# One attention and mixture-of-experts kernel: a ninth column in the gate, integer rank sums, single indirect transfers in two steps, and later weight splits

## The chip, the core and the metric

One NeuronCore of a Trainium2 chip runs the whole program. The metric is the device time of one execution in microseconds. TensorE (PE) multiplies matrices, VectorE (DVE), ScalarE (ACT) and GpSimd (POOL) work element by element, SyncE (SP) issues the plain transfers, and GpSimd issues the indirect ones (scatter and gather by a list of row numbers).

## The reference, cut to what matters

A decaying linear attention over 4 sequences of 768 positions with 8 heads of 48 features gives 3072 rows of 384 features. Each row goes to the one of 8 experts with the largest logit, in order of arrival, up to the capacity of 768 rows an expert, and comes back weighted with the softmax probability of that expert.

```python
state = w * state + k[t] v[t]^T ;  x[t] = r[t] (state_before + u k[t] v[t]^T)
logits = x @ w_gate ;  e = argmax(logits)
z = exp(logits - max) ;  gate = z[e] / (z.sum() + 1e-09)
out[i] = gate[i] * (relu(x[i] @ w1[e]) @ w2[e])      # if the expert still has room
```

At the largest logit z is 1, so the gate is the reciprocal of the sum of z plus 1e-09.

## The kernel before, in words

**Attention.** The 3072 rows are 24 tiles of 128 positions, 6 for each sequence. The loop over `i` (lines 621 to 695) is a software pipeline written out by hand: the order of the calls is the order of the instructions on each engine, and nothing reorders them. Step `i` computes the scores of tile `i + 1` (line 525), masks them (529), scales the keys of tile `i + 3` (511, one product over both halves of the transposed loads), multiplies on GpSimd (495), mixes (81, 83), pulls the tile's logits out (93, 94), updates the state (537, 547), and computes the values of tile `i` (559, 568). ScalarE scales the identity with the bonus of tile `i + 2` (506), copies the values out (572) and writes finished rows into a row buffer (111, 112). There are three row buffers, one for each group of tiles in turn. The last step of a sequence has no state update.

**Routing.** Tiles are routed in groups of two, the last two tiles alone (`GROUPS`, line 33). `route` (125 to 167) is a generator in three parts, and `advance` runs one part at a time. Part one finds the first largest logit and subtracts the maximum. Part two takes the exponential on ScalarE, sums ranks by matmul and adds the group's counts to `lane` on GpSimd (152). Part three (160 to 166) multiplies rank and one-hot mark, sums them into a float, casts to the integer `slot`, sums z, adds 1e-9 and takes the reciprocal. The group's tiles then join `todo`, and `scatters(n)` issues for the first n of them an indirect transfer on GpSimd's queue, which writes 128 rows of 400 words into the sorted array `xsd` in HBM. A step issues one, so a tile is scattered four steps after its values.

**Experts.** Nine sets: the first expert's rows in two halves of 208 (`SETS`, line 26), then one set of 416 for each other expert. `gather(k)` reads a set's rows back, 104 rows an instruction; `xtrans` transposes them on TensorE (300) and splits them into a high and a low part (304 on ScalarE, 305 on VectorE). `layer1` has 8 blocks of 9 matmuls (317 to 319) with a Relu on ScalarE (322) and its low part on VectorE (323) behind each; `layer2` has 3 blocks of 24 matmuls (334 to 336) and a copy (337). The first half of the first expert may use only rows of the first 16 tiles (`SNAP`), so its gather can run before the loop ends. Its first layer's blocks 0 to 3 (called `first` to `fourth`) stand between the last routing parts.

**Weights.** `wstream` is a generator too: each `next(ws)` fetches raw weights on SP's queue into one of four buffers and splits one piece, high part on ScalarE (250), low part on VectorE (251). Pieces 0 to 5 are the first layer's (512 wide), 6 to 13 the second layer's (384 wide). The second expert's weight buffers take the place of the attention's tiles, among them the row buffers that the scatters read.

**Flags.** `flags` (201 to 215) is nine short VectorE instructions and a cast; its result decides at the very end whether a branch for rare inputs runs.

## Time and profile before

| what | value |
|---|---|
| median of three runs | 390.99 us (390.31 to 391.17) |
| the profiled execution's own time | 391.63 us |
| its span (first to last instruction) | 389.9 us |
| mean granted TensorE clock | 0.986 |
| busy: PE, DVE, ACT, POOL | 373.2, 241.3, 204.0, 138.5 us |
| HBM read, written | 52.58 MB, 10.03 MB |

The profile is of one execution, which took 0.64 us more than the median. A busy time counts pipelined instructions as a whole, so a high share of TensorE doesn't say that it runs at its peak. The granted clock is the share of full speed that TensorE was given. In a timeline a row says when an instruction (or a run of like ones, with their count) began, how long it took, the engine, the line, the operation, what it writes and reads, and in brackets how long the engine stood idle before it and what ended that. The engine named there is the last one by the profile; where it had long been done, another wait ended the idle time.

### The profile page before, as it was taken

Reading aid. Unit: us, or ns where it says so; the run is one execution under the profiler, and the core shown is the slowest. Engines: PE = TensorE matmul, PEld = TensorE weight load, DVE = VectorE, ACT = ScalarE, POOL = GpSimd, SP = SyncE. Lnnn points to the kernel's source line nnn. Section 1 sums busy time; section 2 is a strip of 40 time slices with the busy share of each in tenths; the row PEclk is TensorE's granted clock in tenths of the full one; section 3 lists DMA queues with packets and bytes.
Section 4 is the critical chain, followed back from the end, with each engine's and each line's share of the span. In section 5 each row is a group of like instructions: output and inputs, shape, how many; then the busy total and the mean of one; then the engine's idle time right before and its main releaser. Section 6 shows DMA issues by size and latency. Waiting matters only on the chain.

```text
span 389.9 us, 9402 instructions
## 1 busy us (share of the span) xinstructions
PE 373.2 (96%) x3569; PEld 336.3 (86%) x3570; DVE 241.3 (62%) x615; ACT 204.0 (52%) x565; POOL 138.5 (36%) x199
## 2 busy tenths in 40 slices
PE   8999999999999888999999999999999999999993
PEld 3678787787786777999999999999999999999992
DVE  6899999999996656735546546545545645643310
ACT  3668896778787424616525525525625624622301
POOL 7124656575554237402502602602602601201203
PEclk9999999999999996999999999999999999999998
DMA  7848878687812555642743643643644644400102
GB/s 299 329 140 285 282 233 305 233 287 245 262 64 72 151 178 160 183 129 73 209 129 110 197 135 110 185 137 118 187 131 132 185 129 134 137 3 16 43 3 71
DMA packets 20950, 62.51 MB, mean 160 GB/s; under 512 B 3996, under 2 KB 4132, under 8 KB 20896
## 3 DMA queue, kind: packets, MB, share of 16 engines
q1 hardware_dynamic: 15120, 46.74, 38.3%
q0 software_dynamic: 5632, 14.56, 11.6%
q8 instruction: 30, 0.49, 0.5%
q10 hardware_dynamic: 144, 0.52, 0.4%
q14 instruction: 24, 0.20, 0.2%
HBM read 52.58 MB, written 10.03 MB: 161 GB/s over the span
## 4 chain that ended last, share of the span: by engine, by line
PE 60%; issue 14%; DVE 13%; ACT 8%; POOL 2%; DMA 1%; POOLq 1%; ACTq 0%; DVEq 0%
PE a L317 8%; PE a L318 8%; PE a L319 7%; PE b L334 7%; PE b L336 7%; PE b L335 7%; ACT s L506 5%; DVE s L529 4%; PE y L568 3%; PE a L525 2%; PE warm L463 2%; PE yp L350 2%; POOL out L342 2%; PE tp L300 2%; DVE dm L511 2%
## 5 line engine op out<-in xcount | busy, mean ns | idle before, releaser
L342 POOL DMA_INDIRECT out<-yo,ids x32 | 32.4, 1013 | 163.2 <-ACT yo L341 161.6
L317 PE MATMUL a<-xh,ws 128*128 128x416 f32 (+1 forms) x216 | 74.7, 346 | 0.1
L334 PE MATMUL b<-hh,ws 128*128 128x416 f32 (+2 forms) x208 | 72.5, 348 | 2.2 <-ACT hh L322 2.2
L322 ACT ACTIVATE hh<-a 128x416 fp32r<-128x416 f32 (+1 forms) x72 | 34.6, 480 | 72.8 <-PE a L319 69.4
L319 PE MATMUL a<-xh,ws 128*128 128x416 f32 (+1 forms) x216 | 72.1, 334 | 0.0
L318 PE MATMUL a<-xl,ws 128*128 128x416 f32 (+1 forms) x216 | 71.9, 333 | 0.0
L335 PE MATMUL b<-hl,ws 128*128 128x416 f32 (+2 forms) x208 | 70.8, 340 | 0.2 <-DVE hl L323 0.2
L336 PE MATMUL b<-hh,ws 128*128 128x416 f32 (+2 forms) x208 | 70.6, 339 | 0.0
L251 DVE TENSOR_TENSOR ws<-wr,ws 128x384 fp32r<-128x384 f32 (+1 forms) x112 | 67.1, 615 | 5.3 <-ACT ws L250 5.0
L323 DVE SCALAR_TENSOR_TENSOR hl<-a,hh 128x416 fp32r<-128x416 f32 (+1 forms) x72 | 39.0, 542 | 46.3 <-ACT hh L322 35.3
L506 ACT ACTIVATE s<-eye,l 128x128 f32<-128x128 f32 x168 | 53.8, 392 | 18.4 <-DVE l L94 18.2
L250 ACT CAST ws<-wr 128x384 fp32r<-128x384 f32 (+1 forms) x112 | 60.2, 557 | 5.6 <-DMA xsd<-xr,slot 5.6
L337 DVE COPY yt<-b 128x416 f32<-128x416 f32 (+2 forms) x26 | 14.2, 545 | 66.7 <-PE b L336 64.5
L495 POOL TENSOR_TENSOR P<-dm 112x512 f32<-112x512 f32 x21 | 26.8, 1276 | 48.0 <-PE a L525 13.8
L334 PEld LDWEIGHTS b<-hh,ws 128*128 128x128 f32 x208 | 40.4, 194 | 2.6 <-ACT hh L322 2.4
L317 PEld LDWEIGHTS a<-xh,ws 128*128 128x128 f32 x216 | 40.8, 189 | 0.9 <-issue 0.5
L275 POOL DMA_INDIRECT xg<-xsd,pidx x32 | 35.2, 1101 | 17.4 <-issue 8.1
L318 PEld LDWEIGHTS a<-xl,ws 128*128 128x128 f32 x216 | 40.8, 189 | 0.5 <-DVE xl L305 0.2
L335 PEld LDWEIGHTS b<-hl,ws 128*128 128x128 f32 x208 | 40.3, 194 | 1.1 <-DVE hl L323 0.8
L319 PEld LDWEIGHTS a<-xh,ws 128*128 128x128 f32 x216 | 40.7, 188 | 0.1
L336 PEld LDWEIGHTS b<-hh,ws 128*128 128x128 f32 x208 | 40.3, 194 | 0.3
L304 ACT CAST xh<-tp 128x416 fp32r<-128x416 f32 (+1 forms) x27 | 12.3, 472 | 49.9 <-PE tp L300 44.7
(145 smaller groups left out, 580.4 us busy)
## 6 DMA issues: line engine op xcount, KB each, us to landing
wr<-w SPq DMA_DIRECT2D x24, 512.0 KB
wr<-w SPq DMA_DIRECT2D x32, 384.0 KB
dm<-dmj SPq DMA_DIRECT2D x23, 512.0 KB
bd<-bdc SPq DMA_DIRECT2D x24, 384.0 KB
dm<-dmj ACTq DMA_DIRECT2D x1, 512.0 KB
xg<-xsd,pidx POOLq DMA_INDIRECT x32
out<-yo,ids POOLq DMA_INDIRECT x32
xsd<-xr,slot POOLq DMA_INDIRECT x24
```

Of the source, the lines that this page charges most:

```text
L250: nc.scalar.copy(out=hi, in_=r)
L251: low.append(lambda: nc.vector.tensor_tensor(out=lo, in0=r, in1=hi.bitcast(F32), op=ALU.subtract))
L275: nc.gpsimd.indirect_dma_start(out=xg[k % 2][:, i].bitcast(I32), out_offset=None, in_=xsd[:, :], in_offset=bass.IndirectOffsetOnAxis(ap=pi ...
L317: nc.tensor.matmul(a, lhsT=wh, rhs=xh[:, d, o], start=d == 0, stop=False)
L318: nc.tensor.matmul(a, lhsT=wh, rhs=xl[:, d, o], start=False, stop=False)
L319: nc.tensor.matmul(a, lhsT=wl, rhs=xh[:, d, o], start=False, stop=d == 2)
L323: nc.vector.scalar_tensor_tensor(out=hl[:, f, o], in0=a, scalar=0.0, in1=hh[:, f, o].bitcast(F32), op0=ALU.max, op1=ALU.subtract)
L334: nc.tensor.matmul(y, lhsT=wh, rhs=hh[:, f, o], start=f == 0, stop=False)
L335: nc.tensor.matmul(y, lhsT=wh, rhs=hl[:, f, o], start=False, stop=False)
L336: nc.tensor.matmul(y, lhsT=wl, rhs=hh[:, f, o], start=False, stop=f == 7)
L342: r = nc.gpsimd.indirect_dma_start(out=out[:, :], out_offset=bass.IndirectOffsetOnAxis(ap=ids[k][0][:qo, i:i + 1], axis=0), in_=yo, in_off ...
L506: nc.scalar.mul(out=s[:, h, p], in_=eye, mul=bon)
```

## The change

Part three of `route` sums rank times mark straight into the integer `slot`, so the float `sf` and the cast go. The exponentials lie in the first eight of nine columns of a tile `zb`, two of which are used in turn; the ninth column is set to 1e-9 once, by GpSimd, and the sum runs over nine columns, so the addition goes. In steps 20 and 21 of the loop the place of the scatter is taken by one gather each of the first set's two; the end of step 20 no longer empties `todo` and gathers. Four calls of `next(ws)` behind blocks 4 to 7 of the first set's first layer go, one is put behind the second block of its second layer, and `flags` moves there too. The remaining pieces of the second expert follow in the second half's layers, whose loops already call `next(ws)`. The branch for dropped tokens, which runs only when an expert overflows, copies `slot` back to floats.

```diff
--- before.py
+++ after.py
@@ -61,7 +61,7 @@
         fl = const.tile([1, E + 4], I32, name="fl")
         okw = const.tile([128, 1], BF16, name="okw")
         slot = const.tile([128, NI], I32, name="slot")
-        sf = const.tile([128, NI], F32, name="sf")
+        zb = const.tile([128, 2, 4, E + 1], F32, name="zb")
 
         def disjoint(key, r):
             tc.declare_no_dep(r.ins, group=key, reason="rows of one scatter are rows of no other")
@@ -137,7 +137,8 @@
             nc.vector.tensor_reduce(out=km, in_=key, axis=AX.X, op=ALU.max)
             oh = sm.tile(sh, BF16, tag="oh", name=f"oh{gi}")
             nc.vector.tensor_tensor(out=oh, in0=key, in1=km.unsqueeze(2).broadcast_to(sh), op=ALU.is_equal)
-            z = sm.tile(sh, F32, tag="z", name=f"z{gi}")
+            zz = zb[:, gi % 2, 0:n]
+            z = zz[:, :, 0:E]
             nc.vector.tensor_tensor(out=z, in0=l, in1=mxb, op=ALU.subtract)
             yield 1
             nc.scalar.activation(z, z, AF.Exp)
@@ -158,11 +159,10 @@
                 rank = pen
             ps = sm.tile(sh, F32, tag="ps", name=f"ps{gi}")
             nc.vector.tensor_tensor(out=ps, in0=rank, in1=oh, op=ALU.mult)
-            nc.vector.tensor_reduce(out=sf[:, i0:i0 + n], in_=ps, axis=AX.X, op=ALU.add)
-            nc.vector.tensor_copy(out=slot[:, i0:i0 + n], in_=sf[:, i0:i0 + n])
+            with nc.allow_low_precision(reason="one of eight terms is not zero, a whole number below 2^24"):
+                nc.vector.tensor_reduce(out=slot[:, i0:i0 + n], in_=ps, axis=AX.X, op=ALU.add)
             zs = sm.tile([128, n], F32, tag="zs", name=f"zs{gi}")
-            nc.vector.tensor_reduce(out=zs, in_=z, axis=AX.X, op=ALU.add)
-            nc.vector.tensor_scalar(out=zs, in0=zs, scalar1=1e-9, scalar2=None, op0=ALU.add)
+            nc.vector.tensor_reduce(out=zs, in_=zz, axis=AX.X, op=ALU.add)
             nc.vector.reciprocal(out=xr[:, 0:n, DM + 1], in_=zs)
             todo.extend((i, xr[:, i - i0], nd) for i in range(i0, i0 + n))
 
@@ -269,9 +269,9 @@
 
             ids = {}
 
-            def gather(k):
+            def gather(k, tiles=None):
                 q, m = QT, SETS[k][2]
-                for i in range(m):
+                for i in tiles or range(m):
                     nc.gpsimd.indirect_dma_start(out=xg[k % 2][:, i].bitcast(I32), out_offset=None, in_=xsd[:, :],
                                                  in_offset=bass.IndirectOffsetOnAxis(ap=pidx[:q, k, i:i + 1], axis=0),
                                                  bounds_check=E * NT - 1, oob_is_err=False)
@@ -440,6 +440,7 @@
                     nc.gpsimd.memset(lane[:, 0, e:e + 1], float(e * NT // 128))
                     nc.gpsimd.memset(top[:, e:e + 1], float(e * NT + min(cap, NT)))
                     nc.gpsimd.memset(lim[:, e:e + 1], float(e * NT + min(cap, W1S)))
+                nc.gpsimd.memset(zb[:, :, :, E], 1e-9)
                 ii = sup.tile([128, NI], I32, name="ii")
                 nc.gpsimd.iota(ii, pattern=[[C, NI]], base=0, channel_multiplier=1)
                 nc.gpsimd.tensor_copy(out=idf, in_=ii)
@@ -648,7 +649,10 @@
                     each(scores, i + 1)
                 each(prep_keys, i + 3)
                 each(product, i + 3)
-                scatters(1)
+                if i in (20, 21):
+                    gather(0, [i - 20])
+                else:
+                    scatters(1)
                 c = mix(T[i + 2]["P"] if i + 2 < NI else None, T[i - 1]["xs"], ps1)
                 ct = mixed(c, wk)
                 update(i)
@@ -687,9 +691,6 @@
                     setup_ok(wc)
                 if i == 18:
                     early_places(sm, ps1)
-                if i == 20:
-                    scatters(NI)
-                    gather(0)
                 if i in (9, 13):
                     nc.gpsimd.memset(xg[i == 13], 0.0)
                 T.pop(i - 1)
@@ -735,12 +736,12 @@
             next(ws)
             for f in range(4, 8):
                 layer1(0, f)()
-                next(ws)
-            flags(sm)
             layer2(0, 0, columns(0))
             next(ws)
             gather(2)
             layer2(0, 1, columns(0))
+            next(ws)
+            flags(sm)
             take(1)
             for d in range(3):
                 xtrans(1, d)()
@@ -912,6 +913,8 @@
         def drop():
             with tc.tile_pool(name="dw", bufs=1) as dw:
                 rk = dw.tile([128, NI], F32, name="drk")
+                sf = dw.tile([128, NI], F32, name="dsf")
+                nc.vector.tensor_copy(out=sf, in_=slot)
                 nc.vector.tensor_copy(out=rk, in_=sf)
                 for e in range(1, E):
                     ge = dw.tile([128, NI], F32, tag="dge", name=f"dge{e}")
```

## Rows read from the trace of the kernel before

**Rows 1.** The chain that ended last, its shares by engine.

```profile
PE 60%; issue 14%; DVE 13%; ACT 8%; POOL 2%; DMA 1%; POOLq 1%; ACTq 0%; DVEq 0%
```

**Rows 2.** Timeline of PE, scores: start, us, engine, line, op, out<-in, count [idle before].

```profile
38.52 1.16 PE L525 MATMUL a<-dm 48*128 48x128 f32 x16
...
42.78 1.16 PE L525 MATMUL a<-dm 48*128 48x128 f32 x16
...
56.88 1.16 PE L525 MATMUL a<-dm 48*128 48x128 f32 x16
...
61.61 1.16 PE L525 MATMUL a<-dm 48*128 48x128 f32 x16
...
107.30 1.16 PE L525 MATMUL a<-dm 48*128 48x128 f32 x16
```

**Rows 3.** Timelines of DVE and POOL, line 165 and a memset.

```profile
62.30 1.48 DVE L165 TENSOR_SCALAR zs<-zs 128x2 f32<-128x2 f32 x1
...
81.90 1.48 DVE L165 TENSOR_SCALAR zs<-zs 128x2 f32<-128x2 f32 x1
...
62.32 1.43 POOL L694 MEMSET xg<- 104x1600 f32 x1
```

**Rows 4.** Timeline of DVE, one group's lines 162 to 166.

```profile
51.83 0.17 DVE L162 CAST slot<-sf 128x2 int32<-128x2 f32 x1
...
52.11 0.17 DVE L165 TENSOR_SCALAR zs<-zs 128x2 f32<-128x2 f32 x1
...
52.31 0.17 DVE L166 RECIPROCAL xr<-zs 128x2 f32<-128x2 f32 x1
```

**Rows 5.** Timelines of ACT and PE; windows: busy by engine, granted clock, DMA share, GB/s.

```profile
146.71 0.62 ACT L250 CAST ws<-wr 128x512 fp32r<-128x512 f32 x1 [5.58 <-DMA xsd<-xr,slot]
...
143.61 0.27 PE L334 MATMUL b<-hh,ws 128*128 128x208 f32 x1
...
147.63 0.54 PE L334 MATMUL b<-hh,ws 128*128 128x208 f32 x1 [2.18 <-ACT hh L322]
...
128.00:129.00 1.00, 0.00 (x0) 0.00 (x0) 0.61 (x4) 0.17 (x1) 0.44 (x2) 1.00 0.40 90
...
153.00:154.00 1.00, 1.00 (x7) 1.00 (x7) 0.00 (x0) 0.00 (x0) 0.69 (x2) 0.53 0.81 267
```

**Rows 6.** Timelines of POOL and DVE, lane additions and the keys' product.

```profile
42.78 1.45 POOL L152 TENSOR_TENSOR lane<-lane,oh 128x8 bf16<-128x8 bf16 x2
...
51.70 0.49 POOL L152 TENSOR_TENSOR lane<-lane,oh 128x8 bf16<-128x8 bf16 x2
...
42.95 1.23 DVE L511 TENSOR_TENSOR dm<-dm,ft 112x1024 f32<-112x1024 f32 x1
```

**Rows 7.** Timeline of POOL, gathers and scatters at the loop's end.

```profile
121.83 1.08 POOL L275 DMA_INDIRECT xg<-xsd,pidx  x1 [0.30 <-issue]
...
125.92 1.04 POOL L173 DMA_INDIRECT xsd<-xr,slot  x1 [2.49 <-ACT ws L250]
...
135.05 0.99 POOL L173 DMA_INDIRECT xsd<-xr,slot  x1 [5.75 <-ACT hh L322]
```

**Rows 8.** Timelines of PE, DVE and POOL where the experts begin.

```profile
154.95 0.70 PE L300 MATMUL tp<-idn,xg 104*128 104x104 f32 x6
...
140.41 0.17 DVE L166 RECIPROCAL xr<-zs 128x1 f32<-128x1 f32 x1
...
141.34 1.07 POOL L173 DMA_INDIRECT xsd<-xr,slot  x1 [2.18 <-ACT hh L322]
...
147.34 1.09 POOL L275 DMA_INDIRECT xg<-xsd,pidx  x1 [4.93 <-DMA xsd<-xr,slot]
...
148.73 1.17 POOL L275 DMA_INDIRECT xg<-xsd,pidx  x1 [0.30 <-issue]
```

**Rows 9.** Groups by line and form, line 251: count | busy, mean ns | idle.

```profile
L251 DVE TENSOR_TENSOR ws<-wr,ws 128x512 fp32r<-128x512 f32 x48 | 33.6, 700 | 5.2 <-ACT ws L250 5.0
...
L251 DVE TENSOR_TENSOR ws<-wr,ws 128x384 fp32r<-128x384 f32 x64 | 33.5, 550 | 0.1
```

## The prediction, made before the change was run

> **What bounds the kernel now.** The page's chain of waits comes first: TensorE holds 60% of it, VectorE 13%, ScalarE 8% [rows 1]. So TensorE sets the time in most of the kernel, and a saving on VectorE counts only where VectorE is late. The pieces of that chain in order of time say where: through more than half of the attention loop they are mostly VectorE and ScalarE, then TensorE, and where the experts begin once more a transfer and ScalarE. So there are two stretches to price.
>
> The first stretch is the attention loop. I read its pace from TensorE's timeline: the score matmuls (line 525) open each step. A step that nothing holds up takes 4.73 us (56.88 to 61.61), and one without a state update, every sixth, 4.26 us (38.52 to 42.78) [rows 2]. From 61.61 to 107.30 us there are nine steps, two of the short kind: at the free pace 7 x 4.73 + 2 x 4.26 = 41.63 us, in fact 45.69 us. **4.06 us are excess**, and that is the most TensorE can get back there.
>
> VectorE's timeline shows what it does meanwhile. The addition of 1e-9 (line 165) lasts 1.48 us at 62.30 and again at 81.90; at 52.11 it lasts 0.17. At 62.32 GpSimd starts a memset of 1.43 us, and the addition ends 0.03 us behind it [rows 3, 4]. So VectorE stands still for 1.31 us, twice. From there it is behind: the reading of the pulled row (line 94) comes late, ScalarE's diagonal scalings wait for it, and TensorE's next mixing matmuls wait for the copy behind those.
>
> The second stretch begins at 141 us. ScalarE's first split for the second expert waits 5.58 us until 146.71, for the landing of the last scatter, whose source rows lie where the new weights go. Behind it in ScalarE's order stand the Relus of the first expert's feature blocks 5 to 7, and TensorE waits 2.18 us for block 5 until 147.63. From there a matmul lasts 0.54 us that lasted 0.27 at 143.61 [rows 5], and the granted clock is still 0.53 in the us from 153: the lower level, 1.2 of 2.4 GHz, until about 153.9.
>
> **The change, part by part.**
>
> *Two small instructions less per group of tiles.* Summing ranks straight to integers removes the cast of line 162; the ninth column removes the addition of line 165. From the start of the addition to that of the reciprocal it is 0.20 us (52.11 to 52.31); the cast lasts the same 0.17 and stands in the same kind of chain, so I give it 0.20 too: 0.40 us a group [rows 4]. Five groups pass this part between 61.61 and 107.30 (lines 160 to 166 run once in two steps): 2.0 us. With the two standstills, 2.62 us, VectorE gets 4.6 us free, more than the excess of 4.06. Not all of it comes back. A step that has both a low split and the first part of the routing keeps all its VectorE work, and nothing of it gets shorter; following the order of the three engines through the steps with the rows' durations leaves one wait of about 0.5 us before 107. I take **-3.5 us**. The bounds are -4.06 (all excess) and -1.0, if the standstill only passes to another instruction (a rival, below). Groups before 61 us save nothing: there the next masking waits for the scores anyway. Groups after 107 us finish where TensorE has no excess, except the last two, which count below.
>
> The memset of the ninth column is one more small one in GpSimd's setup, beside the first loads, and a ninth element in a short reduction is nothing I can see; both at 0. The copy added in the branch for dropped tokens is not on the path that runs.
>
> There is a price on the other side. VectorE now reaches its big product (line 511) 0.40 us sooner, where GpSimd adds the lane counts. At 51.70 two such additions take 0.49 us; at 42.78 they take 1.45 us, because that product began at 42.95 [rows 6]. There GpSimd waited. If VectorE waits instead, it loses at most what is left of the additions, about 0.2 us a group, 1.0 us in five; I take 0, since the only meeting in these rows went VectorE's way, and keep 1.0 for the range. The Trainium skill (SBUF — State Buffer, section "Who interferes with whom") says that a VectorE instruction with two SBUF inputs and a GpSimd one that reads SBUF exclude each other, whichever issues first. The rows agree with that for GpSimd as the loser; by that page the additions, issued first here, would win, and the sum would be 1.0 us higher.
>
> *One indirect transfer a step.* The two gathers of the first set move from the end of step 20 to the place of the scatters of steps 20 and 21; four scatters move behind them, and 18 and 19 now go out with 20 and 21 after the loop. In GpSimd's queue there is room: it stands idle for 5.75 us before the scatter of 135.05 us [rows 7], which takes two more issues of 1.0 us each, and the lane additions and later scatters behind them wait for nothing new. The gathers come no later than before. It costs something if the scatters of 18 and 19, done by about 131.7 us in this order, land late: the last tile's rows go into the same buffer, at some 135.3 us. With the 3.0 us of a gather's landing (121.83 + 1.08 to the scatter at 125.92, which had to wait for it) they are in time [rows 7]; the last scatter took 4.93 us from its issue's end to the next issue [rows 8]. So 0 to 1.3 us, and I take 0, for the transfers before 135 us are the nearer ones.
>
> *Splits and flags later.* Without four splits between the Relus, the wait of 2.18 us and its half clock go. TensorE runs on through blocks 4 to 7 and the second layer of the first half. What is late next is the gather of the other half. The last scatter starts 0.76 us behind its reciprocal's end (140.41 + 0.17 to 141.34), and the gathers follow at 147.34 and 148.73 [rows 8]. Two groups ahead of that reciprocal get shorter by 0.4 us each, so all this comes some 0.8 us sooner: the second gather issued by 149.1 (it took 1.17 us), landed by 152.1 with the 3.0 us above. TensorE gets through the 48 matmuls of the second layer's two blocks by 149.0 (15 of them ran from 143.61 until the wait began at 145.45, 0.12 us each [rows 5]), and then waits some 3.1 us instead of 2.2, before the transposes, which start at 152.1 instead of 154.95 [rows 8]: **-2.85 us**. If the clock falls again in that wait, some 6.3 us at half rate follow, as they did from 147.63 to 153.9: **+3.15 us**, less about 0.3 that hide behind the waits for the split inputs. The part is worth **0**. The splits that arrive in the second half's first layer are wide ones in place of narrow ones, 0.70 against 0.55 us on VectorE [rows 9]; for four of them that is 0.6 us, hidden behind TensorE at half rate; without that cover 0.6 is the price. The flags' instructions move into VectorE's wait for the gather. A raw weight is fetched when a split frees its buffer, so SP issues some fetches later; the splits that read them have moved back as well.
>
> **Sum.** The profiled execution took 391.63 us, 0.64 above the median of 390.99. 391.63 - 3.5 + 0 = 388.1; against the median 387.5.
>
> **Rivals.**
> 1. *Forecast, 0.58:* attention gains 3.5, the clock falls a second time: 387.5.
> 2. *The clock holds, 0.20.* In the us from 128 TensorE is idle and the granted clock stays 1.00 [rows 5]; if the new wait is short enough, or falls well, the 2.85 us are kept: 384.6. Against it: the new wait is longer than the one that lost the clock. The Trainium skill (TensorE: Matmul & The Clock Gate, section "HAM oscillation — how this bites in real kernels") describes waits for data after each of which matmuls start at the low rate again. By that page the forecast stands and this gain does not come.
> 3. *The standstill moves, 0.15.* The change would then not do what it is meant to: the reciprocal, behind the addition, also has one small input and may meet the memset. It would start at about 62.1, before the memset's 62.32, and no reciprocal of this trace is long, which speaks against it. Then only the 2.0 us of the short instructions are free, at worst less the 1.0 for GpSimd's additions; I price the case there: attention gains 1.0, 390.0.
> 4. *Slower, 0.07: the clock stays low.* The place is the first layer of the second half, eight blocks of nine matmuls. ScalarE and VectorE now have a split behind each block's Relu there; if TensorE has to wait for them block by block, the clock may not rise until the layer is through. At the low level its 72 matmuls take 72 x 0.24 = 17.3 us, which costs 8.65 - 0.3 in place of 2.85: -3.5 - 2.85 + 8.35 = +2.0, 393.0. It decides from 13.3 us at the low level (half of it, less 0.3, is 6.35). Against it: VectorE's wide split of 0.70 us is well below the 2.2 us of a block at half rate, and the clock of before rose again although the first matmuls behind the wait came with gaps.
>
> **Numbers.** A difference of about 0.2%, 0.8 us, is what can be told from none. The likeliest case gives 387.5; with two of its bounds on top (1.0 for the additions, 0.6 for wider splits) it reaches to 389.1. The range takes in rival 2 at the low end and most of the way to rival 3: 384.4 to 389.6. Faster by over 0.2% are cases 1 and 2 and part of 3: 0.86; within 0.2%: 0.09; slower: 0.05.
>
> **What would show it.** The score matmuls keep a pace near 4.73 us from 61 to 107 us and reach 107.30 some 3.5 us earlier; no VectorE instruction of this part lasts over 0.3 us. ScalarE's Relus of blocks 4 to 7 follow each other, TensorE's wait before block 5 is gone, and a new one stands before the transposes of the second half, ended by the gather, with a granted clock of 0.5 after it. I am wrong if the pace stays near 5 us, if the clock stays 1.00 (rival 2) or stays low for over 13 us (rival 4).

## The result, and the profile after

The changed kernel took **386.91 us** (median of six runs, 386.06 to 387.71), the kernel before, run beside it, 390.65 us (six runs, 389.50 to 391.72): a ratio of **0.9905, 95% interval 0.9881 to 0.9929**. The prediction was 387.5 in 384.4 to 389.6. The profiled execution of the changed kernel took 386.67 us, its span is 385.0; that of before has 391.63 and 389.9, and stands 1.0 us above the median of these six, so that the two traces differ by more (4.9 us of span) than the medians (3.7). Line numbers of the changed kernel are one higher than before's in the attention loop. Of the twelve executions of the kernel without the scatter in step 23 (below), three took over 393 us at a mean clock of 0.971 to 0.977; its median and ratio are those of the other nine.

TensorE's timeline of the changed kernel, at the two scores that answer to the last two of [rows 2]:

```profile
61.58 1.16 PE L526 MATMUL a<-dm 48*128 48x128 f32 x16
...
105.35 1.16 PE L526 MATMUL a<-dm 48*128 48x128 f32 x16
```

The nine steps between take 43.77 us instead of 45.69. So 1.92 us of the 4.06 us excess are gone, not 3.5. The last of the nine steps begins in before at

```profile
101.70 1.16 PE L525 MATMUL a<-dm 48*128 48x128 f32 x16
```

and lasts 5.60 us, until 107.30, for a free 4.73. It takes 5.60 to 5.62 us in all fourteen traces of this document, whatever was edited: 0.9 us of the excess are untouched. What holds this step was not tested. The same comparison at further places (us, start of the row named):

| place | before | after | gain so far | by the prediction |
|---|---|---|---|---|
| scores at the end of the nine steps | 107.30 | 105.35 | 1.95 | 3.5 |
| the loop's last scores | 122.36 | 119.40 | 2.96 | 3.5 |
| block 4 of the first half's first layer | 139.52 | 136.27 | 3.25 | 3.5 |
| second half, first matmul | 155.71 | 148.84 | 6.87 | 6.35 |
| transposes of the next set | 164.23 | 158.90 | 5.33 | 3.5 |
| span | 389.9 | 385.0 | 4.9 | 3.5 |

The place of [rows 3], the second of the two standstills, in VectorE's timeline of the changed kernel, and GpSimd's beside it:

```profile
80.00 0.16 DVE L165 TENSOR_REDUCE zs<-zb 128x2 f32<-128x18 f32 x1
80.20 0.17 DVE L166 RECIPROCAL xr<-zs 128x2 f32<-128x2 f32 x1
80.28 1.20 DVE L512 TENSOR_TENSOR dm<-dm,ft 112x1024 f32<-112x1024 f32 x1
...
83.28 1.43 DVE L251 TENSOR_TENSOR ws<-wr,ws 128x512 fp32r<-128x512 f32 x1
...
79.98 1.56 POOL L153 TENSOR_TENSOR lane<-lane,oh 128x8 bf16<-128x8 bf16 x2
81.48 1.43 POOL L695 MEMSET xg<- 104x1600 f32 x1
82.88 1.27 POOL L496 TENSOR_TENSOR P<-dm 112x512 f32<-112x512 f32 x1
```

The two long additions of [rows 3] are gone, and no reciprocal is long. But a standstill is back: the low split of 83.28 lasts 1.43 us (700 ns in the mean of [rows 9]) and ends behind GpSimd's product (82.88 + 1.27 = 84.15). That product stands behind the memset, and the memset behind the two lane additions, which last 1.56 us here and 0.49 at 51.70 [rows 6], because VectorE's big product began together with the second of them.

Where the experts begin, the rows that answer to [rows 5] and [rows 8]: timelines of ScalarE, GpSimd and TensorE of the changed kernel.

```profile
142.96 1.14 ACT L250 CAST ws<-wr 128x512 fp32r<-128x512 f32 x2 [2.05 <-DMA xsd<-xr,slot]
...
143.57 1.09 POOL L275 DMA_INDIRECT xg<-xsd,pidx  x1 [4.79 <-issue]
144.97 1.09 POOL L275 DMA_INDIRECT xg<-xsd,pidx  x1 [0.30 <-issue]
...
146.82 0.31 PE L300 MATMUL tp<-idn,xg 104*128 104x104 f32 x1 [0.94 <-DMA xg<-xsd,pidx]
148.11 0.67 PE L300 MATMUL tp<-idn,xg 104*128 104x104 f32 x5 [0.99 <-DMA xg<-xsd,pidx]
148.84 0.36 PE L317 MATMUL a<-xh,ws 128*128 128x208 f32 x1
```

The wait of 2.18 us for block 5 is gone. In its place TensorE waits 0.94 and 0.99 us for the two gathers, 1.93 us in all (predicted: 3.1); the second lands 2.05 us behind its issue's end (144.97 + 1.09 to 148.11, when the transposes that need it start; predicted: 3.0). Then the clock falls. Windows of the changed kernel (the column ahead of the DMA share is the granted clock):

```profile
149.00:150.00 1.00, 0.95 (x7) 0.78 (x8) 0.76 (x3) 0.27 (x2) 0.70 (x2) 1.00 0.94 366
150.00:151.00 1.00, 1.00 (x9) 1.00 (x8) 0.19 (x1) 0.56 (x2) 0.69 (x2) 0.71 0.55 167
151.00:152.00 1.00, 1.00 (x7) 1.00 (x6) 0.87 (x2) 0.29 (x1) 0.97 (x1) 0.50 0.52 138
...
153.00:154.00 1.00, 1.00 (x8) 1.00 (x6) 0.77 (x2) 0.17 (x1) 0.70 (x2) 0.58 0.10 37
154.00:155.00 1.00, 1.00 (x12) 1.00 (x10) 0.41 (x2) 0.85 (x2) 0.84 (x1) 1.00 0.56 176
```

From about 150.4 to 153.8 us TensorE has the lower level, 3.4 us (before: 147.1 to 153.9).

One thing in the two traces belongs to no part of the prediction: ScalarE's copy of the values, `xs`, begins up to 1.4 us after the matmuls that it reads. Timelines of the changed kernel in the loop's last step:

```profile
127.57 1.08 PE L569 MATMUL y<-s,bd 128*48 128x128 f32 x16
...
128.43 0.98 POOL L173 DMA_INDIRECT xsd<-xr,slot  x1 [0.31 <-DVE gw L288]
...
130.06 0.65 ACT L573 COPY xs<-y 128x256 f32<-128x256 f32 x2 [2.73 <-PE y L569]
```

The matmuls end at 128.65, `xs` starts at 130.06, and a second indirect transfer of GpSimd began just ahead of that end. In the trace of before this is there three times (1.34, 0.97 and 1.02 us, in steps 20 to 22), in the changed kernel once. The first of the three in before, whose matmuls end at 116.72:

```profile
115.64 1.08 PE L568 MATMUL y<-s,bd 128*48 128x128 f32 x16
118.06 0.65 ACT L572 COPY xs<-y 128x256 f32<-128x256 f32 x2 [1.27 <-PE a L525]
```

It stands ahead of the loop's last scores, and it is the 1.0 us that the second line of the table has on top of the first.

### The profile page after: what moved, and what is told of

Its sections match the earlier page's. It is cut to its first block, busy times and chain, and to the rows that moved or that the text cites. A ratio compares the mean times of both kernels' runs of the same rounds, so it can differ in the third digit from the quotient of the medians.

```text
span 385.0 us, 9378 instructions
## 1 busy us (share of the span) xinstructions
PE 370.3 (96%) x3569; PEld 335.3 (87%) x3570; DVE 236.5 (61%) x589; ACT 204.4 (53%) x565; POOL 143.9 (37%) x200
## 4 chain that ended last, share of the span: by engine, by line
PE 46%; issue 12%; POOL 2%; DMA 1%; POOLq 1%; ACT 0%; DVE 0%; ACTq 0%
PE a L318 8%; PE a L317 7%; PE a L319 7%; PE b L334 7%; PE b L335 7%; PE b L336 7%; PE yp L350 2%; POOL out L342 2%; PE tp L300 2%; DMA xg<-xsd,pidx 1%; POOLq L757 0%; DMA xsd<-xr,slot 0%; POOLq L933 0%; DVE ws L251 0%; ACT ws L250 0%
## 5 line engine op out<-in xcount | busy, mean ns | idle before, releaser
L317 PE MATMUL a<-xh,ws 128*128 128x416 f32 (+1 forms) x216 | 75.6, 350 | 0.1
L318 PE MATMUL a<-xl,ws 128*128 128x416 f32 (+1 forms) x216 | 72.8, 337 | 0.0
L319 PE MATMUL a<-xh,ws 128*128 128x416 f32 (+1 forms) x216 | 72.7, 336 | 0.0
L334 PE MATMUL b<-hh,ws 128*128 128x416 f32 (+2 forms) x208 | 71.4, 343 | 0.0
L336 PE MATMUL b<-hh,ws 128*128 128x416 f32 (+2 forms) x208 | 69.5, 334 | 0.0
L335 PE MATMUL b<-hl,ws 128*128 128x416 f32 (+2 forms) x208 | 69.4, 334 | 0.0
L317 PEld LDWEIGHTS a<-xh,ws 128*128 128x128 f32 x216 | 41.5, 192 | 0.9 <-DVE xl L305 0.3
L319 PEld LDWEIGHTS a<-xh,ws 128*128 128x128 f32 x216 | 41.5, 192 | 0.4
L318 PEld LDWEIGHTS a<-xl,ws 128*128 128x128 f32 x216 | 41.6, 192 | 0.3 <-DVE xl L305 0.2
L334 PEld LDWEIGHTS b<-hh,ws 128*128 128x128 f32 x208 | 39.4, 190 | 0.1
L336 PEld LDWEIGHTS b<-hh,ws 128*128 128x128 f32 x208 | 39.2, 188 | 0.3
L335 PEld LDWEIGHTS b<-hl,ws 128*128 128x128 f32 x208 | 39.3, 189 | 0.0
```

What stands on the lines that cost most here:

```text
L317: nc.tensor.matmul(a, lhsT=wh, rhs=xh[:, d, o], start=d == 0, stop=False)
L318: nc.tensor.matmul(a, lhsT=wh, rhs=xl[:, d, o], start=False, stop=False)
L319: nc.tensor.matmul(a, lhsT=wl, rhs=xh[:, d, o], start=False, stop=d == 2)
L334: nc.tensor.matmul(y, lhsT=wh, rhs=hh[:, f, o], start=f == 0, stop=False)
L335: nc.tensor.matmul(y, lhsT=wh, rhs=hl[:, f, o], start=False, stop=False)
L336: nc.tensor.matmul(y, lhsT=wl, rhs=hh[:, f, o], start=False, stop=f == 7)
```

## The experiments

Twelve kernels, in three sets of four. The kernels of a set ran on one chip, each with the kernel before beside it, whose medians were 388.48 us in the first set, 390.97 in the second and 390.88 in the third. Times are compared as ratios to before within a set. The changed kernel itself ran again in the second set alone; the kernels of the third are held against its ratio there. Places in the traces are told in us since the scores of step 4 (33.85 in before, 33.81 in the changed kernel), since executions begin up to 0.7 us apart.

### First set: each part alone

The ninth column alone:

```diff
+            zz = zb[:, gi % 2, 0:n]
+            z = zz[:, :, 0:E]
...
-            nc.vector.tensor_reduce(out=zs, in_=z, axis=AX.X, op=ALU.add)
-            nc.vector.tensor_scalar(out=zs, in0=zs, scalar1=1e-9, scalar2=None, op0=ALU.add)
+            nc.vector.tensor_reduce(out=zs, in_=zz, axis=AX.X, op=ALU.add)
```

> The kernel before with the ninth column alone (the addition of 1e-9 is gone, the cast stays). Theory (the addition met GpSimd's memset twice and stood still for 1.3 us each time; without it nothing else does): the score matmuls of before's 107.30 come 1.2 to 1.9 us sooner, and the whole is 1.0 to 1.9 us shorter. Rival (the standstill passes to the reciprocal, which now starts about when the memset does): at least one reciprocal of over 1 us, and at most 0.5 us gained.

The whole numbers alone:

```diff
-            nc.vector.tensor_reduce(out=sf[:, i0:i0 + n], in_=ps, axis=AX.X, op=ALU.add)
-            nc.vector.tensor_copy(out=slot[:, i0:i0 + n], in_=sf[:, i0:i0 + n])
+                nc.vector.tensor_reduce(out=slot[:, i0:i0 + n], in_=ps, axis=AX.X, op=ALU.add)
```

> The kernel before with the ranks summed straight to whole numbers alone (the cast is gone, the addition stays). Theory (what counts is whether the addition meets the memset): the addition starts 0.2 us sooner, near 62.1 us, just ahead of the memset of 62.32, so the first standstill goes and the second may go; 0.5 to 1.5 us gained. Rival (only the 0.2 us of each instruction count, and the addition still meets the memset): additions of 1.3 to 1.5 us stay at both places, 0 to 0.4 us gained.

Measured: the column alone 385.90 us, 0.9932 (0.9915 to 0.9948), the whole numbers alone 385.73 us, 0.9931 (0.9918 to 0.9944). **Either instruction alone is worth 2.6 to 2.7 us**, more than the theories had (1.0 to 1.9 and 0.5 to 1.5 us). The scores at the end of the nine steps come 73.45 us after those of step 4 in before, 70.79 with the column alone (2.66 sooner), 71.15 with the whole numbers alone (2.30), and 71.54 with both in the changed kernel (1.91): in this stretch both together bring less than one. The chips don't differ here: before's 73.45 is repeated to 0.03 us by the next two kernels of this set, and the changed kernel's 71.54 by its second trace, on the second set's chip. Where the addition stays, it lasts 0.17 us at both places: it is through 0.05 us before the memset begins. VectorE's and GpSimd's timelines with the whole numbers alone:

```profile
61.60 0.17 DVE L164 TENSOR_SCALAR zs<-zs 128x2 f32<-128x2 f32 x1
...
80.04 0.17 DVE L164 TENSOR_SCALAR zs<-zs 128x2 f32<-128x2 f32 x1
...
61.82 1.44 POOL L693 MEMSET xg<- 104x1600 f32 x1
...
80.26 1.44 POOL L693 MEMSET xg<- 104x1600 f32 x1
```

Why one is better than two is read from the place of the second standstill. VectorE's and GpSimd's timelines with the column alone:

```profile
80.18 0.17 DVE L167 RECIPROCAL xr<-zs 128x2 f32<-128x2 f32 x1
80.26 1.20 DVE L513 TENSOR_TENSOR dm<-dm,ft 112x1024 f32<-112x1024 f32 x1
...
83.06 0.69 DVE L252 TENSOR_TENSOR ws<-wr,ws 128x512 fp32r<-128x512 f32 x1
...
79.77 0.49 POOL L154 TENSOR_TENSOR lane<-lane,oh 128x8 bf16<-128x8 bf16 x2
80.19 1.43 POOL L696 MEMSET xg<- 104x1600 f32 x1
81.60 1.28 POOL L497 TENSOR_TENSOR P<-dm 112x512 f32<-112x512 f32 x1
```

The lane additions are through (0.49 us) when the big product begins at 80.26; GpSimd's product ends at 82.88, and the split at 83.06 finds it gone. With both instructions removed the big product begins 0.30 us behind the start of the additions (80.28 against 79.98), the second addition waits for it, and GpSimd is 1.1 us later with all that follows (places since the scores of step 4).

One transfer a step alone:

```diff
-                scatters(1)
+                if i in (20, 21):
+                    gather(0, [i - 20])
+                else:
+                    scatters(1)
...
-                if i == 20:
-                    scatters(NI)
-                    gather(0)
```

> The kernel before with one indirect transfer a step alone. The prediction gave this part 0. Theory from the comparison of the two traces (ScalarE's copy of the values, xs, starts late where two GpSimd transfers stand back to back beside the last values matmuls; with the gathers in steps 20 and 21 fewer of them do): the score matmuls of step 23 (122.36 before) come 0.8 to 1.2 us sooner, and the time is 0.7 to 1.3 us shorter. Rival (the prediction): the attention loop ends where it did, no difference.

Measured: 388.33 us, 0.9994 (0.9985 to 1.0003), no difference. The rival holds. On this chip no `xs` of steps 18 to 23 is late by more than 0.2 us, neither here nor in the next kernel, whose loop is that of before. So the late copies don't come from the code of the loop alone.

The moved splits and flags alone:

```diff
             for f in range(4, 8):
                 layer1(0, f)()
-                next(ws)
-            flags(sm)
...
             layer2(0, 1, columns(0))
+            next(ws)
+            flags(sm)
```

> The kernel before with the moved splits and flags alone. Theory (in the changed kernel this part and the earlier gathers work together; here the gathers come when they came before, the second one issued by 149.9 us and landed 2.0 to 3.0 us later): the wait for feature block 5 goes, TensorE waits some 5 us before the transposes, which start at 152 to 153 us instead of 154.95, the granted clock falls again behind that wait and costs 1.7 to 3.2 us: between 1.2 us gained and 0.3 lost. Rival 1 (the part is worth the same alone, 2.1 us as in the changed kernel): 2 us gained. Rival 2 (the clock holds): 2.9 us gained.

Measured: 387.63 us, 0.9974 (0.9965 to 0.9983): 1.0 us gained, within the theory's bounds. The second half's first matmul comes 3.3 us sooner than in the kernel with the single transfers (116.02 against 119.34 since the scores of step 4), and its first layer, until the next transposes, takes 10.76 us instead of 8.43. TensorE's waits for the gathers are those of the changed kernel, somewhat longer, and 2.7 us in all where the theory had 5:

```profile
147.01 0.31 PE L300 MATMUL tp<-idn,xg 104*128 104x104 f32 x1 [1.35 <-DMA xg<-xsd,pidx]
...
148.69 1.13 PE L300 MATMUL tp<-idn,xg 104*128 104x104 f32 x5 [1.36 <-DMA xg<-xsd,pidx]
```

By its half-microsecond windows the granted clock is 0.5 from 148.1 to 154.9 us, 6.8 us.

### Second set: the changed kernel again, the memsets, the gap

> The changed kernel itself once more, as the control for the runs beside it. If the parts add up as the first four runs have them (1.9 us of attention for both small instructions together, 0.2 for the order of the transfers, 0.85 for the late splits), 2.9 us less than before; 3.7 us if the first comparison holds as it stands. A late start of ScalarE's copy of the values (xs), 1 us and more behind the last values matmuls, is to be looked for: if it belongs to the order of the transfers it is there again in step 23, if to single executions it may be anywhere or nowhere.

Measured: 387.77 us, 0.9915 (0.9886 to 0.9943), which agrees with the first comparison. The trace repeats itself: 71.51 us to the end of the nine steps, and `xs` of step 23 late by 1.41 us once more. But the clock stayed at its lower level for 6.8 us where the first trace has 3.4, and the second half's first layer took 10.94 us in place of 10.06. All its executions say the same by their mean granted clock: of the twelve, four at 0.991 or 0.992 took 386.1 to 386.7 us, seven at 0.987 or 0.988 took 387.2 to 389.9, and one at 0.997 took 386.3. So its median depends on how many executions got the long stretch.

The kernel before with nothing but the memsets moved (before's steps 3 and 5 take 4.73 and 4.26 us, the free pace):

```diff
-                if i in (9, 13):
-                    nc.gpsimd.memset(xg[i == 13], 0.0)
+                if i in (3, 5):
+                    nc.gpsimd.memset(xg[i == 5], 0.0)
```

> The kernel before with both small instructions kept and the two memsets of GpSimd moved from steps 9 and 13 to steps 3 and 5, where the next masking waits for the scores anyway. Theory (the two standstills are the whole gain of attention): no addition over 0.4 us near 62 and 82 us, the score matmuls of 107.30 come 2.0 to 2.7 us sooner, 2.0 to 2.7 us gained in all, as much as by either instruction alone. Rival (the instructions' own time is the gain, 0.4 us a group): the standstill is only half of the 4.06 us excess, 0.5 to 1.3 us gained.

Measured: 389.71 us, 0.9981 (0.9961 to 1.0001); against the theory that is too little, against the rival not enough to tell. TensorE's timeline says why:

```profile
62.07 1.16 PE L525 MATMUL a<-dm 48*128 48x128 f32 x16
...
105.62 1.16 PE L525 MATMUL a<-dm 48*128 48x128 f32 x16
```

The nine steps take 43.55 us instead of 45.69: 2.14 us without taking any instruction away, so **the standstills alone hold 2.14 of the 4.06 us**. But the steps ahead of them now take 0.68 us more (28.44 against 27.76 since the scores of step 4): VectorE's scaled keys of line 517 stand still at 45.91 (1.54 us for 0.55), so the slack there did not cover it.

The same edit in the changed kernel:

> The changed kernel with the memsets in steps 3 and 5. Theory (in the changed kernel one standstill came back: behind the memset of 81.48 GpSimd's product runs until 84.15, and VectorE's low split of 83.28 waits for it, 1.43 us in place of 0.70): that split lasts 0.7 us, the score matmuls of 105.35 come 0.6 to 1.2 us sooner, 0.6 to 1.2 us faster than the changed kernel. Rival (the waits come from the lane additions that push the product back, not from the memset): 0 to 0.2 us.

Measured: **385.64 us, 0.9863 (0.9847 to 0.9880)**, 0.5% under the changed kernel beside it, and the lowest ratio of the twelve, from four executions. VectorE's and GpSimd's timelines at the place of the returned standstill:

```profile
83.59 0.68 DVE L251 TENSOR_TENSOR ws<-wr,ws 128x512 fp32r<-128x512 f32 x1
...
80.30 1.55 POOL L153 TENSOR_TENSOR lane<-lane,oh 128x8 bf16<-128x8 bf16 x2
81.93 1.28 POOL L496 TENSOR_TENSOR P<-dm 112x512 f32<-112x512 f32 x1
```

The additions still last 1.55 us, but without the memset the product is through at 83.21 and the split takes 0.68 us. The nine steps take 42.89 us; 0.23 us are lost ahead of them. That is the theory's 0.6 us and no more. The other part is another stage: in this trace the clock did not fall at all. Windows:

```profile
148.00:149.00 1.00, 0.89 (x7) 0.51 (x6) 0.91 (x4) 0.78 (x3) 0.69 (x2) 1.00 0.72 198
...
152.00:153.00 1.00, 1.00 (x12) 1.00 (x10) 0.80 (x2) 0.54 (x2) 0.70 (x2) 1.00 0.17 46
...
155.00:156.00 1.00, 0.00 (x0) 0.00 (x0) 0.70 (x2) 0.64 (x2) 0.70 (x2) 1.00 0.90 358
```

Its waits ahead of the transposes, 0.96 and 0.85 us, are almost those of the changed kernel. In this execution the held clock gave little: the layer took 10.35 us, since TensorE stood idle in the us from 155. Three of the four executions have a mean clock of 0.997 or 0.998, against one of the changed kernel's twelve. Whether moving the memsets makes the clock hold, or the four had luck, these runs don't tell; what they show for the edit itself is the 0.6 us. Waits of TensorE from 148 to 165 us:

```profile
PE a L317 <- DVE hl L323: 1.4, 2, 1.2
```

ScalarE is behind that: its Relus, which VectorE's `hl` waits for, start up to 2.9 us after the end of the block that they read (VectorE itself stands 0.30 us for the one behind which TensorE waits longest). In the four traces of the first set each of the eight starts 0.03 or 0.04 us behind its block.

The third block of the second layer moved into the wait for the gathers:

```diff
             flags(sm)
+            layer2(0, 2, columns(0))
             take(1)
...
-                        layer2(k, d, columns(1) if k == 1 and d < 2 else slice(0, WL))
+                        layer2(k, d, columns(1) if k == 1 else slice(0, WL))
```

> The changed kernel with the third block of the second layer of the first half put ahead of the transposes of the second half (24 matmuls of 0.11 us, 2.7 us), in place of beside the same block of the second half later. Theory (TensorE stands 1.9 us ahead of the transposes for the gathers, and the clock falls because of it): the wait goes, the transposes start 0.3 to 0.9 us later, the clock stays at 1.00, 2.0 to 3.5 us faster than the changed kernel. Rival 1 (the clock falls all the same): 0.7 to 1.5 us faster. Rival 2 (the block was hidden beside other waits where it stood): no gain, or up to 0.9 us lost.

Measured: 386.44 us, 0.9895 (0.9854 to 0.9936), an interval that holds the changed kernel's ratio: no difference that can be told among executions from 384.6 to 390.3 us. In the trace the clock stayed at 1.00, as the theory has it, one wait of 0.89 us for a gather is left, and the transposes started 1.5 us later than in the changed kernel beside it; ScalarE's late Relus (up to 2.4 us) made TensorE wait in the layer here too.

### Third set: splits into the gap, everything together, the late copies

Two more splits ahead of the transposes (the changed kernel with this):

```diff
             layer2(0, 0, columns(0))
             next(ws)
+            next(ws)
...
             layer2(0, 1, columns(0))
             next(ws)
+            next(ws)
             flags(sm)
```

> The changed kernel with two more of the second expert's splits in the gap ahead of the transposes: one more behind each of the two blocks of the second layer (four in all, six in the layer behind become fewer by two). Theory (the second half's first layer lasts 10.1 to 10.9 us in the changed kernel against 8.5 before, because VectorE has a low split behind each block; at full clock TensorE waits 1.2 us for it, at the low level that wait is hidden): the layer lasts 8.5 us plus what the clock takes, no wait for VectorE's hl in it, 0.5 to 1.5 us faster than the changed kernel. Rival (the clock alone sets that layer): the same 10 to 11 us, 0 to 0.2 us.

Measured: 387.76 us, 0.9917 (0.9896 to 0.9939): the rival holds, nothing gained. The clock was low for 6.8 us, all of it within the layer, and the layer took 11.46 us. That is 72 matmuls of 0.11 us, 8.0, and half of 6.8: the clock alone. With the clock low this run can't show whether the splits would bound the layer at full clock. But the expectation took its wait of 1.2 us for `hl` from the trace with the early memsets, and there VectorE itself was waiting for a late Relu, not for its splits: that reading was wrong.

All of it together, with the memsets in steps 3 and 5, the two more splits and the block moved (the diffs above on the changed kernel):

> The changed kernel with the memsets in steps 3 and 5, the four splits ahead of the transposes and the third block of the second layer ahead of them. If each is worth what the runs so far have it (about 2.0 us for the memsets, 0.5 to 0.8 for the block, 0.5 to 1.5 for the splits): 3 to 4 us faster than the changed kernel, 0.978 to 0.984 of before. Rival (they fill the same wait): no better than the memsets alone, 0.986.

Measured: 387.69 us, 0.9894 (0.9864 to 0.9924): no gain over the changed kernel that can be told. The six executions fall apart by the clock: two at 0.997 took 385.2 and 385.6 us, four at 0.986 or 0.987 took 387.2 to 388.3. In the traced one, of the slower four, the loop is that of the early memsets (70.90 us to the end of the nine steps), but the wait ahead of the transposes is back, and the clock fell behind it for 6.8 us. GpSimd's and TensorE's timelines:

```profile
144.28 1.09 POOL L275 DMA_INDIRECT xg<-xsd,pidx  x1 [0.31 <-issue]
...
150.16 1.12 PE L300 MATMUL tp<-idn,xg 104*128 104x104 f32 x5 [2.06 <-DMA xg<-xsd,pidx]
```

The second gather landed 4.8 us behind its issue's end, 2.05 in the changed kernel and 2.7 with the two splits alone. Earlier splits free weight buffers sooner, and the fetches into them start sooner; in the us from 145 to 147 the transfers move 197 and 309 GB/s here, 199 and 331 with the two splits alone, 141 and 69 in the changed kernel. So the fetches do run beside the gather. But with the two splits alone it landed in 2.7 us beside as much traffic, so the traffic by itself doesn't set the delay, and what does stays open.

The changed kernel without the scatter in step 23, which goes out behind the loop:

```diff
-                else:
+                elif i != 23:
                     scatters(1)
```

> The changed kernel without the scatter in step 23 (it goes out with those behind the loop). ScalarE's copy xs of that step started 1.41 us behind the last values matmul in three executions, each time with a second GpSimd transfer starting 0.2 us ahead of that matmul's end. Theory (the second transfer holds it up): xs starts at the end of the matmuls, 1.0 to 1.4 us faster than the changed kernel, on a chip that shows the delay at all; on one like that of the first four runs, which showed none, no difference. Rival (the delay belongs to the step, not to the transfer): xs is late here too, no gain.

Measured: 388.63 us, 0.9954 (0.9929 to 0.9980): no gain. ScalarE's, TensorE's and GpSimd's timelines:

```profile
127.25 0.65 ACT L573 COPY xs<-y 128x256 f32<-128x256 f32 x2 [1.35 <-PE y L569]
131.00 0.27 ACT L88 COPY ct<-c 128x128 f32<-128x128 f32 x1 [2.63 <-issue]
...
128.38 0.42 PE L83 MATMUL c<-xs,wgz 128*32 128x128 f32 x8
...
127.43 0.97 POOL L173 DMA_INDIRECT xsd<-xr,slot  x1 [0.30 <-DVE xl L305]
128.70 0.97 POOL L173 DMA_INDIRECT xsd<-xr,slot  x1 [0.31 <-ACT xr L112]
129.98 0.97 POOL L173 DMA_INDIRECT xsd<-xr,slot  x1 [0.30 <-issue]
```

The copy is prompt (its matmuls end at 127.24), as the theory has it, but the delay has moved: the copy `ct`, whose matmuls end at 128.80, starts at 131.00, beside three transfers in a row. By the last scatter nothing is left of the gain.

The kernel before with one transfer a step, the edit of the first set on another chip:

> The kernel before with one indirect transfer a step alone, once more. On the first chip it changed nothing (0.9994), and its trace showed no late xs. In the first traces of both kernels, and in those of the runs of the second call, late copies stood behind second transfers: three times in before, once in the changed kernel. Theory (on such a chip the order of the transfers is worth the difference, two delays of 1.0 to 1.3 us): 1.0 to 2.5 us faster than before if before's late copies are there again, none if this chip is like the first. Rival (the delays have nothing to do with the transfers): no difference on any chip.

Measured: 391.81 us, 1.0035 (1.0016 to 1.0054), slower by 1.4 us where the first set had 0.9994. The trace has two late copies, by 1.6 and 1.2 us, at 123.3 and 132.8 us, both with two transfers beside them. The theory's gain did not come, and the rival's "no difference" is missed by a little: the order of the transfers shifts which copies are late.

## Why the prediction came out right, point by point

The time and the way, faster through attention with the clock falling a second time (rival 1), came out; the terms did not. Three errors offset one another, and that the sum came within 0.6 us is luck.

- **Two small instructions less, forecast -3.5, measured -1.9.** The step that failed is the price that I took as 0, for the lane additions that VectorE's big product now meets. The meeting went as I said, GpSimd lost and the product kept its 1.2 us. But I priced VectorE's loss at that meeting only, not what GpSimd does next: its second addition waits 1.0 us, the memset and the product behind it move back, and VectorE's low split pays 0.73 us for it (1.43 against 0.70). One instruction less avoids that meeting and is worth 2.3 to 2.66 us. With the memsets moved and both instructions gone, the nine steps take 42.89 us: so the meeting costs 43.77 - 42.89 = 0.88 of the 1.58 us by which the term was too good. The other 0.70 is the assumption that one wait of about 0.5 us is all that remains (4.06 - 3.5 = 0.56): 42.89 - 41.63 = 1.26 us of excess stay. Some 0.9 of them stand in the step of 5.60 us, which no edit moved: taking the whole 4.06 us as what these instructions could bring back was that much too high. The Trainium skill (SBUF — State Buffer, section "Who interferes with whom") has the instruction that is issued first win the port. At 80.28 both begin in the same hundredth of a microsecond and GpSimd's loses, so these rows do not decide the rule; the first addition, alone ahead of it, did run through.
- **The standstills as the source of the excess: right for about half of it.** Moving the memsets alone brings the nine steps 2.14 of 4.06 us, with all instructions in place.
- **Small edits at 0 and the order of the transfers at 0: right on the first set's chip** (0.9994), where a late landing cost nothing. On the other chip the same part measured 1.0035, with ScalarE's late starts in its trace, which the prediction doesn't have. The 1.3 us that the changed kernel gained between the nine steps and block 4 lie where these late copies are, three in one trace and one in the other; no run shows them as a merit of the order.
- **Splits and flags later, forecast 0, measured -1.0** (0.9974) alone. The terms were -2.85 for the transposes and +3.15 - 0.3 for the clock. The first is 3.3, because the gather lands 2.0 to 2.5 us behind its issue in these two kernels, not 3.0. The second is 2.3 us in that kernel (10.76 against 8.43 us for the layer) and 1.5 in the changed kernel's first trace, where the lower level lasted 3.4 us. I had taken it over whole from the stretch before; but the length of that stretch is no constant of the kernel.
- **The wider splits, 0 behind their cover, 0.6 without it: the cover was not theirs.** In the two traces with the clock held, ScalarE's lateness set the layer; in the one with two more splits and the clock low for 6.8 us nothing did but the clock (8.0 + 3.4 against 11.46).

Of the rivals: the clock held in two of the twelve traces, but 2.85 us did not come of it, for the layer took 9.9 and 10.35 us all the same. The executions at 0.997 of the kernel with everything together were 1.6 to 3.1 us faster than its others, so there a held clock went with about what rival 2 had; in the changed kernel it held in one of twelve. The Trainium skill (TensorE: Matmul & The Clock Gate, section "HAM oscillation — how this bites in real kernels") describes a kernel whose matmuls start at the low rate again after every wait for data. Here the clock fell behind 0.94 and 0.99 us of waiting in the changed kernel and not behind 0.96 and 0.85 in the one with early memsets, so the traces agree with it in some executions and not in others, and the length of the waits by itself does not tell. The standstill did move, as rival 3 says, but to the low split, not to the reciprocal, once, and for about half its time. The clock that stays low did not come: no stretch was longer than 6.8 us. That the edits did what they say is seen in the rows: no cast, no addition.

The changed kernel did not run on the first set's chip. With 1.9 us from its own trace, 0.2 for the transfers (which can't be told from none) and 1.0 for the splits, the terms add up to 3.1 us, less than the 3.7 of the first comparison and within its interval (0.9929 is 2.8 us).

## What to carry to other kernels

Where two engines stand in each other's way, shortening one moves the next meeting: follow the loser's queue as far as the next instruction that the winner shares with it, and try one of two savings before both. If the collision is the cost, moving the colliding instruction may be worth as much as removing the one that it hits, provided that its new place really has slack. And a gain ahead of a wait counts only as far as the wait, and the clock behind it, let it through: the edits of the gap ahead of the transposes moved rows by microseconds, and the medians by little; which executions held the clock moved them as much.

## What the runs showed that was not expected

- **The lower level of TensorE's clock came in three lengths: 6.8 us, 3.4 us and none.** By the granted clock in half-microsecond windows, nine of the fourteen traces have 6.8 us at 1.2 GHz in this stage, three have 3.4, two have none; the changed kernel itself had 3.4 in one execution and 6.8 in another.
- **ScalarE starts late in the ten traces outside the first set, and not in that set's four.** The twelve copies `xs` of steps 20 to 23 that are late by 0.97 us or more all start 0.5 to 0.7 us after the end of the second of two indirect transfers, wherever their matmuls ended. In seven of these ten, Relus of the second half's first layer start 0.7 to 2.9 us behind their block, while GpSimd issues one indirect transfer after another; taking one transfer away moved such a delay. What it is, and whether it makes the 2.4 us between the chips' medians of the kernel before, stays open.
- **A wait without a name is not a delay.** From 200 to 380 us the views of these ten traces put four waits of the Relus down to nothing ("issue"). The waits of ScalarE in that stretch, in the changed kernel's first trace and with the column alone (engine, line, what for: sum, times, longest):

```profile
ACT hh L322 <- PE a L319: 55.4, 44, 4.9
ACT hh L322 <- issue: 2.7, 4, 0.7
...
ACT hh L323 <- PE a L320: 58.1, 48, 4.9
```

There are 48 waits of 58.1 us in all in both: the one trace names TensorE for every one, the other for 44. And in all fourteen traces no Relu of the later sets starts more than 0.04 us behind its block. So nothing is late in this stretch; only starts set against the end of what they read, as above, show a delay.
